# A fused recurrent-attention and feed-forward kernel: input products leave PSUM by a copy and run a block ahead, softplus made from a tanh, another order of steps

## The chip, the cores and the metric

The kernel runs on one core of a Trainium2 chip, as one launch. The time is that of the device for one execution, in microseconds (us). A core has five engines that run their own queues in order: TensorE (PE, matrix products into PSUM; PEld is its weight load), VectorE (DVE), ScalarE (ACT, activation functions read from a table that must be loaded), GpSimd (POOL) and SyncE (SP, here the queue that starts the DMA transfers). PSUM is the memory that TensorE writes to; SBUF is the working memory.

## The reference

```python
def _attn_ref(q, k, v, alpha):          # each (4, 8, 768, 48) float32
    for t in range(S):
        state = alpha[:, :, t, :, None] * state + einsum('bhd,bhe->bhde', k[:, :, t], v[:, :, t])
        y[:, :, t] = einsum('bhd,bhde->bhe', q[:, :, t], state)
def _moe_ref(x, w_in, w_out):           # x = y as (3072, 384); w_in (384, 2048); w_out (2048, 384)
    h = x @ w_in
    sp = np.maximum(h, 0.0) + np.log1p(np.exp(-np.abs(h)))
    g = h * erf(sp)
    return g @ w_out
```

A gated linear recurrence gives x; the feed-forward part takes a product, multiplies it by the erf of its own softplus, and takes a second product.

## The kernel before

**Attention** is done in 24 chunks of 64 steps, each for two of the four batch entries. `ld` starts seven transfers (alpha, k, q in two halves each, v) on SP. `a1` makes the running products of alpha with one scan on VectorE (line 168), `a2` their reciprocals (ScalarE: a check, Ln, Exp; VectorE: a Newton step), `a3` scales k and q, `a4` transposes k (`pn`, line 199) and multiplies q by k (`pS`, line 210), `a5` makes the output (`py`, line 238) and the update of the state T (`pu`, line 249), and splits the output into two halves x_hi and x_lo of the feed-forward's input (lines 286 and 287). The step named `a6` is empty. There are two sets of raw tiles for alpha, q and k, used in turn, and two raw_v.

**The feed-forward part** works on 12 blocks of 256 tokens; two chunks fill one block's x. The 2048 columns are four groups g of 512, and a group is two halves. For a half, `H` takes 18 products (three for each of three slices of the input and two columns of 128: hi by hi, lo by hi, hi by lo; line 323) into a PSUM bank `ph` (two banks); ScalarE reads the bank twice, exp into `w` (line 334, with a running sum into `hflags`) and a copy into `hs` (line 335). `L1` makes s = ln(1 + w), the softplus, and then exp(-ln s), a first reciprocal; `L2` refines it on VectorE (lines 348, 349). `E` loads the gelu table, takes the gelu of all four groups (line 354) and loads the table of logarithm and exp again: erf comes from the gelu and the reciprocal. `Z` multiplies and adds (lines 359, 360). `O` splits a half into gh and gl (a cast on VectorE or a copy on ScalarE, lines 371 and 373, and a subtraction, line 374) and takes 12 products (line 382) into the two accumulators `acc` of the block; there are two `acc` banks in all. `out` copies the accumulators to `o`, one buffer (line 390), and starts the transfers to the output.

The weights come in 28 pieces (`wi_n`, `wo_n`) that are staged in buffers of the pools of `hs` and `s`, converted on ScalarE and VectorE and kept in SBUF as hi and lo halves.

**What sets the order.** The steps are traced in an order written out by hand: START once, ORDER in a loop, TAIL once. `H_0_1@1` is the second half of group 0 of the next block, `Z_0@-1` belongs to the block before; in `a1_0` and `ld_1` the number counts chunks from the loop's first chunk. START holds the first block to its end, seven chunks and the second block's H and L; nine rounds of ORDER and TAIL follow. A planner of the framework then sorts each engine's instructions by that order as a priority and by its own costs, and places tiles into the pools' buffers; an instruction that needs a buffer waits until its last reader is done. Instructions given to `tab` can't be moved across a table load (`new_phase`, line 127). So a table load divides ScalarE's work into two phases: one for gelu, one for logarithm and exp, with the attention's Ln and Exp in the latter. In total 25 tables are loaded.

`general()` is a slow path behind a flag for inputs out of range; it does not run with this data.

Of the kernel before, what the change touches and what calls it, by code (L numbers as in the profile page):

```python
# [14 lines left out]
AMIN = 1e-18  # L15
# [6 lines left out]
RMAX = 1e17  # L22
HMAX = 1e17
SAT = 4.0
RT2 = 2.0**0.5
# [5 lines left out]
    for z in (  # L31
# [13 lines left out]
    )  # L45
# [4 lines left out]
def gla_moe(ctx: ExitStack, tc: tile.TileContext, q, k, v, alpha, w_in, w_out, out):  # L50
# [21 lines left out]
    xp = fast.enter_context(tc.tile_pool(name="xp", bufs=2))  # L72
    keep_s = fast.enter_context(tc.tile_pool(name="keep_s", bufs=NG))
    keep_h = fast.enter_context(tc.tile_pool(name="keep_h", bufs=NG + 1))
    keep_w = fast.enter_context(tc.tile_pool(name="keep_w", bufs=NG + 1))
    tmp = fast.enter_context(tc.tile_pool(name="tmp", bufs=1))
# [4 lines left out]

    raws = []
    for n in range(2):

        ra = raw.tile([P, NP * NI, 1 + TC], F32, name=f"raw_a{n}")
        rq, rk = (raw.tile([P, NP, NI, TC], F32, name=f"raw_{nm}{n}") for nm in "qk")
        e = nc.vector if n == 0 else nc.gpsimd
        for t, fill in ((ra, 1.0), (ra[:, :, 0], 0.0), (rq, 0.0), (rk, 0.0)):
            e.memset(t, fill)
        raws.append((ra, rq, rk))  # L90

# [4 lines left out]
    for i in range(NI):  # L96
# [3 lines left out]
        )  # L100
    fixed = const.tile([P, 5], F32, name="fixed")
    floor, bhi, bsat, bone, ones = (fixed[:, n : n + 1] for n in range(5))
    for t, val in ((floor, AMIN), (bhi, -AHI), (bsat, SAT), (bone, 1.0 + 2.0**-23), (ones, 1.0)):
        nc.gpsimd.memset(t, val)
    NS = M * CPB
    flags = const.tile([P, NS, 2], F32, name="flags")
    nc.gpsimd.memset(flags, 0.0)

    hflags = const.tile([P, NBLK * NG * 2], F32, name="hflags")
    nc.gpsimd.memset(hflags, 0.0)  # L110

# [34 lines left out]
    class Chunk:  # L146
# [6 lines left out]
        def ld(self):  # L153
            self.ra, self.rq, self.rk = raws[self.n % 2]
            self.vv = raw.tile([P, NI * NP * HD + H * D], F32, name="raw_v", tag="raw_v", bufs=2)
            for t, src in ((self.ra[:, :, 1:], alpha), (self.rk, k), (self.rq, q)):
                t = t if src is alpha else t.rearrange("p a i t -> p (a i) t")
                for par in range(2):
                    nc.sync.dma_start(
                        out=t[par * HD : par * HD + D],  # L160
                        in_=src[self.m, self.c, par].rearrange("d a i t -> d (a i) t"),
                    )
            nc.sync.dma_start(out=self.vv, in_=v[self.m, self.c])
# [104 lines left out]

    pools = SimpleNamespace(xp=xp, s=keep_s, h=keep_h, w=keep_w, tmp=tmp, gp=gp, acc=ps_acc, ph=ps_h, flags=hflags)

    class Moe:
# [38 lines left out]
        def H(self, g, half):  # L310
            x_hi, x_lo = self.x
            if half == 0:
                self.hs[g] = self.pl.h.tile([P, GT * TB], F32, name="hs", tag="hs")
                self.w[g] = self.pl.w.tile([P, GT * TB], F32, name="w", tag="w")
            ph = self.pl.ph.tile([P, 512], F32, name="ph", tag="h")
# [11 lines left out]
            sl = slice(half * 512, (half + 1) * 512)  # L327
            w = self.w[g][:, sl]
            if self.pl.flags is None:
                nc.scalar.activation(w, ph, AF.Relu, scale=-1.0, bias=bsat)  # L330
                nc.scalar.activation(w, w, AF.Exp, scale=-1.0, bias=bsat)
            else:
                n = (self.n * NG + g) * 2 + half
                tab(nc.scalar.activation(w, ph, AF.Exp, accum_out=self.pl.flags[:, n : n + 1]))  # L334
            nc.scalar.activation(self.hs[g][:, sl], ph, AF.Copy)  # L335

        def L1(self, g):
            w = self.w[g]
            s = self.pl.s.tile([P, GT * TB], F32, name="s", tag="s")
            tab(nc.scalar.activation(s, w, AF.Ln, bias=bone))  # L340
            tab(nc.scalar.activation(w, s, AF.Ln))  # L341
            tab(nc.scalar.activation(w, w, AF.Exp, scale=-1.0))  # L342
            self.s[g] = s

        def L2(self, g):
            w, s = self.w[g], self.s[g]
            t = self.pl.tmp.tile([P, GT * TB], F32, name="t", tag="tmp")
            nc.vector.tensor_tensor(out=t, in0=s, in1=w, op=ALU.mult)  # L348
            nc.vector.scalar_tensor_tensor(out=w, in0=t, scalar=2.0, in1=w, op0=ALU.subtract, op1=ALU.mult)  # L349

        def E(self):
            new_phase(GELU)
            for s in self.s:
                tab(nc.scalar.activation(s, s, AF.Gelu, scale=RT2))  # L354
            new_phase(LNEXP)

        def Z(self, g):
            s, w, h = self.s[g], self.w[g], self.hs[g]
            nc.vector.tensor_tensor(out=s, in0=s, in1=w, op=ALU.mult)  # L359
            nc.vector.scalar_tensor_tensor(out=h, in0=s, scalar=RT2 / 2, in1=h, op0=ALU.add, op1=ALU.mult)  # L360

# [25 lines left out]
        def out(self):  # L387
            for tt in range(2):
                o = self.pl.gp.tile([P, DM], F32, name="o", tag="o", bufs=1)
                nc.scalar.activation(o, self.acc[tt][:, :DM], AF.Copy, scale=-RT2)  # L390
                nc.sync.dma_start(out=out[bass.ds(self.toks[tt], P), :], in_=o)
# [40 lines left out]
    def general():  # L432

        with ExitStack() as es:
# [47 lines left out]
            rows = part.rearrange("g b t a r e -> g (b t) (a r e)")  # L482
            pl = SimpleNamespace(xp=one, s=one, h=two, w=one, tmp=one, gp=two, acc=acc, ph=ph, flags=None)
            with tc.For_i(0, NT, TB) as tok:
# [10 lines left out]
                for g in range(NG):  # L495
                    m.H(g, 0)
                    m.H(g, 1)
                    m.L1(g)
                    m.L2(g)
                    nc.scalar.activation(m.s[g], m.s[g], AF.Gelu, scale=RT2)  # L500
                    m.Z(g)
# [9 lines left out]
    for n in range(NBLK):  # L511
        m, j = divmod(n, CPB // 2)
        moes.append(Moe(n, [(m * NI + i) * S + j * P for i in range(NI)], pools))

    def run(order, c0, b0):

        for step in order:
# [7 lines left out]
            elif name[0] in "la":  # L525
                if c0 + arg[0] < len(chunks):
# [5 lines left out]
                    else:  # L532
                        getattr(ch, name)()
            elif b0 + int(rel or 0) < NBLK:
                getattr(moes[b0 + int(rel or 0)], name)(*arg)

    run(START, 0, 0)
    for i in range(2, NBLK - 1):
        run(ORDER, 2 * i + 3, i)
    run(TAIL, 2 * NBLK, NBLK - 1)  # L540


    top = const.tile([P, 3], F32, name="top")
    nc.vector.tensor_reduce(
        out=top[:, 0:2], in_=flags.rearrange("p n two -> p two n"), op=ALU.max, axis=mybir.AxisListType.X
    )
    nc.vector.tensor_reduce(out=top[:, 2:3], in_=hflags, op=ALU.max, axis=mybir.AxisListType.X)
    count = const.tile([P, 1], F32, name="count")
    nc.vector.tensor_scalar(out=count, in0=top[:, 0:1], scalar1=RMAX, scalar2=None, op0=ALU.is_ge)
    for n, lim in ((1, 0.0), (2, HMAX)):  # L550
        nc.vector.scalar_tensor_tensor(
            out=count, in0=top[:, n : n + 1], scalar=lim, in1=count, op0=ALU.is_gt, op1=ALU.add
        )
    pf = ps_at.tile([P, 512], F32, name="pf", tag="at")
# [62 lines left out]
```

## Time and profile before

| | us |
|---|---|
| median of three runs | 612.34 |
| lowest and highest | 604.37, 614.47 |
| the profiled execution | 614.45 |
| its span, first to last instruction | 612.7 |
| TensorE busy in the span | 532.7 (87%) |
| TensorE's weight load busy | 507.3 (83%) |
| VectorE busy | 485.8 (79%) |
| ScalarE busy | 476.7 (78%) |
| GpSimd busy | 4.3 (1%) |

The mean granted clock of TensorE is 0.966. A matmul's row shows its whole passage, so that rows of neighbouring matmuls overlap, and the busy time of a group is more than its share of the engine; the distance from start to start is what one costs in a dense row. The first gelu load of each block's output stands at 89.49, 139.68, 177.39, 224.66, 271.18, 316.45, 361.59, 408.54, 453.55, 500.81, 548.63 and 577.70 us: these cut the span into START (two stretches), nine rounds of ORDER and TAIL's two stretches. In a group's row there stand the busy time, the mean duration in ns, and after the second bar the idle time of its engine just before it with what ended it.

### The profile page before, as it was taken

To read this page: it belongs to the slowest core of one execution; us is meant where nothing else is said; L and a number is where in the kernel's file an instruction comes from. 1 tells how busy PE (TensorE), PEld (TensorE's weight loads), DVE (VectorE), ACT (ScalarE), POOL (GpSimd) and SP (SyncE) were. 2 spreads that over 40 slices of the span, in tenths; PEclk is the share of its full clock that TensorE was granted. 3 is DMA by queue.
4 is the path that set the end of the run, shared out by engine and by line. 5 is a ranking of instruction groups with operands and counts; after the bars stand their busy time and mean duration, and the time that the engine had idled before them with its cause. 6 is when DMAs were issued, how large, how long until landed. Compare 5 with 4: busy or idle time off the path is not lost.

```text
span 612.7 us, 17112 instructions
## 1 busy us (share of the span) xinstructions
PE 532.7 (87%) x7386; PEld 507.3 (83%) x7386; DVE 485.8 (79%) x690; ACT 476.7 (78%) x847; POOL 4.3 (1%) x23
## 2 busy tenths in 40 slices
PE   0588498998998998998999998999998998999994
PEld 0468397897988987987988988988988987989984
DVE  6889999899988588678689588589588588549781
ACT  4458988889986887787887886887886787679941
POOL 2000000000000000000000000000000000000000
PEclk9999697999998998999999998999998998999998
DMA  9765523414122122111122122122122010000000
GB/s 250 234 229 170 152 77 111 134 39 110 40 71 71 27 71 71 40 57 58 40 71 71 27 72 71 27 71 71 27 71 71 1 32 28 1 2 27 1 27 30
DMA packets 36371, 43.65 MB, mean 71 GB/s; under 512 B 21952, under 2 KB 25024, under 8 KB 36288
## 3 DMA queue, kind: packets, MB, share of 16 engines
q1 hardware_dynamic: 36288, 42.48, 23.7%
q8 instruction: 60, 0.98, 0.7%
q14 instruction: 23, 0.19, 0.1%
HBM read 37.75 MB, written 4.72 MB: 69 GB/s over the span
## 4 chain that ended last, share of the span: by engine, by line
ACT 38%; PE 29%; DVE 22%; DMA 6%; issue 4%; SPq 0%; DVEq 0%; ACTq 0%
PE acc L382 15%; PE ph L323 11%; ACT w L334 5%; ACT s L354 5%; ACT s L340 4%; ACT hs L335 4%; DMA out_dram<-o 4%; ACT w L341 3%; DVE t L348 3%; ACT w L342 3%; DVE A L168 3%; ACT gh L373 3%; ACT L127 3%; ACT r L176 2%; DVE w L349 2%
## 5 line engine op out<-in xcount | busy, mean ns | idle before, releaser
L323 PE MATMUL ph<-x_hi,wi_hi 128*128 128x256 f32 x576 | 164.9, 289 | 14.4 <-ACT x_hi L286 12.9
L323 PE MATMUL ph<-x_hi,wi_lo 128*128 128x256 f32 x576 | 163.6, 285 | 0.7 <-DVE wi_lo L395 0.7
L323 PE MATMUL ph<-x_lo,wi_hi 128*128 128x256 f32 x576 | 164.0, 285 | 0.0
L382 PE MATMUL acc<-wo_hi,gh 128*128 128x384 f32 x384 | 137.6, 359 | 21.5 <-ACT o L390 16.1
L382 PE MATMUL acc<-wo_hi,gl 128*128 128x384 f32 x384 | 133.0, 349 | 1.2 <-DVE gl L374 1.2
L382 PE MATMUL acc<-wo_lo,gh 128*128 128x384 f32 x384 | 133.3, 348 | 0.0
L323 PEld LDWEIGHTS ph<-x_hi,wi_hi 128*128 128x128 f32 x576 | 109.7, 192 | 17.3 <-ACT x_hi L286 14.5
L323 PEld LDWEIGHTS ph<-x_lo,wi_hi 128*128 128x128 f32 x576 | 110.6, 192 | 1.4 <-DVE x_lo L287 1.2
L323 PEld LDWEIGHTS ph<-x_hi,wi_lo 128*128 128x128 f32 x576 | 110.4, 192 | 1.4 <-DVE wi_lo L395 1.2
L374 DVE TENSOR_TENSOR gl<-hs,gh 128x512 fp32r<-128x512 f32 x96 | 65.2, 687 | 46.7 <-ACT gh L373 46.5
L334 ACT ACTIVATE w<-ph 128x512 f32<-128x512 f32 x96 | 57.6, 601 | 57.1 <-PE ph L323 55.6
L382 PEld LDWEIGHTS acc<-wo_hi,gh 128*128 128x128 f32 x384 | 75.2, 196 | 26.8 <-ACT o L390 18.9
L348 DVE TENSOR_TENSOR t<-s,w 128x1024 f32<-128x1024 f32 x48 | 58.6, 1221 | 31.9 <-ACT w L342 31.9
L382 PEld LDWEIGHTS acc<-wo_hi,gl 128*128 128x128 f32 x384 | 74.9, 196 | 2.4 <-DVE gl L374 2.3
L382 PEld LDWEIGHTS acc<-wo_lo,gh 128*128 128x128 f32 x384 | 75.7, 197 | 0.0
L373 ACT ACTIVATE gh<-hs 128x512 fp32r<-128x512 f32 x72 | 45.3, 630 | 25.9 <-PE acc L382 25.6
L359 DVE TENSOR_TENSOR s<-s,w 128x1024 f32<-128x1024 f32 x48 | 57.7, 1219 | 2.3 <-ACT s L354 2.3
L349 DVE SCALAR_TENSOR_TENSOR w<-t,w 128x1024 f32<-128x1024 f32 x48 | 58.5, 1218 | 0.7
L360 DVE SCALAR_TENSOR_TENSOR hs<-s,hs 128x1024 f32<-128x1024 f32 x48 | 57.6, 1218 | 0.1
L335 ACT ACTIVATE hs<-ph 128x512 f32<-128x512 f32 x96 | 56.1, 598 | 0.0
L340 ACT ACTIVATE s<-w,fixed 128x1024 f32<-128x1024 f32 x48 | 55.5, 1159 | 0.1
L341 ACT ACTIVATE w<-s 128x1024 f32<-128x1024 f32 x48 | 51.4, 1074 | 0.2
(68 smaller groups left out, 745.2 us busy)
## 6 DMA issues: line engine op xcount, KB each, us to landing
raw_v<-in_v_dram SPq DMA_DIRECT2D x24, 448.0 KB, 3.7
wst<-in_moe_w_in_dram SPq DMA_DIRECT2D x12, 512.0 KB, 5.8
wst<-in_moe_w_out_dram SPq DMA_DIRECT2D x16, 384.0 KB, 3.7
raw_a<-in_alpha_dram SPq DMA_DIRECT2D x48, 96.0 KB, 2.9
raw_k<-in_k_dram SPq DMA_DIRECT2D x48, 96.0 KB, 2.2
raw_q<-in_q_dram SPq DMA_DIRECT2D x48, 96.0 KB, 2.4
out_dram<-o SPq DMA_DIRECT2D x24, 192.0 KB, 3.4
```

The source lines that it names most:

```text
L323: nc.tensor.matmul(out=o, lhsT=wt[:, kt, fs], rhs=xt[:, kt, :], start=n == 0, stop=n == 3 * KT - 1)
L334: tab(nc.scalar.activation(w, ph, AF.Exp, accum_out=self.pl.flags[:, n : n + 1]))
L335: nc.scalar.activation(self.hs[g][:, sl], ph, AF.Copy)
L340: tab(nc.scalar.activation(s, w, AF.Ln, bias=bone))
L341: tab(nc.scalar.activation(w, s, AF.Ln))
L348: nc.vector.tensor_tensor(out=t, in0=s, in1=w, op=ALU.mult)
L349: nc.vector.scalar_tensor_tensor(out=w, in0=t, scalar=2.0, in1=w, op0=ALU.subtract, op1=ALU.mult)
L359: nc.vector.tensor_tensor(out=s, in0=s, in1=w, op=ALU.mult)
L360: nc.vector.scalar_tensor_tensor(out=h, in0=s, scalar=RT2 / 2, in1=h, op0=ALU.add, op1=ALU.mult)
L373: nc.scalar.activation(ghf, gg, AF.Copy)
L374: nc.vector.tensor_tensor(out=gl.rearrange("p a t -> p (a t)"), in0=gg, in1=ghf.bitcast(F32), op=ALU.subtract)
L382: nc.tensor.matmul(out=self.acc[tt][:, :DM], lhsT=gt[:, u, ts], rhs=wt[:, f, :], start=f == 0 and n == 0, stop=f == NF - 1 and n == 2,)
```

## The change

- `H` only copies `ph` to `hs`. The exp from PSUM and the `hflags` sum go.
- A new step `U` makes s = tanh(-h/2) from `hs`, 1024 elements at a time, with the table of gelu. `L1` takes ln(0.5 + 0.5 s), which is minus the softplus, then ln(-s) and exp of minus that. `L2`, `Z`, the gelu (now a step `G` for one group) and `out` change signs.
- `E` is gone; the order names the table loads itself, `GELU` and `LN`. In a round, the gelu of block i-1 and the tanh of block i share one phase, the logarithms of block i and the attention have the other.
- Buffers: `s` 5 for 4, `hs` 7 for 5, `w` 4 for 5. One set of raw tiles for alpha, q and k instead of two.
- START ends before the first block's gelu; it holds six chunks, H, U, L1 and L2 of block 0, and six of the eight halves of H of block 1. The loop has eleven rounds, i = 1 to 11; in round i stand H_3 of block i, H_0 to H_2 of block i+1, the attention of chunks 2i+4 and 2i+5 (the x of block i+2), U, L1 and L2 of block i, and G, Z, O and out of block i-1. TAIL is the last block's G, Z, O and out. 26 tables are loaded.

```diff
-        "E@-1 Z_0@-1 O_0_0@-1 O_0_1@-1 a1_0 a2_0 Z_1@-1 O_1_0@-1 a3_0 H_1_0 H_1_1 H_2_0 a4_0 H_2_1 H_3_0 "
-        "Z_3@-1 O_1_1@-1 H_3_1 L1_0 L1_1 Z_2@-1 ld_1 a5_0 a6_0 H_0_0@1 H_0_1@1 L2_0 L2_1 O_2_0@-1 O_2_1@-1 "
-        "O_3_0@-1 L1_2 L2_2 a1_1 a2_1 a3_1 a4_1 O_3_1@-1 L1_3 L2_3 a5_1 a6_1 ld_2 out@-1 ",
+        "GELU a1_0 G_0@-1 G_1@-1 Z_0@-1 H_3_0 G_2@-1 U_0 H_3_1 Z_1@-1 O_0_0@-1 U_2 O_0_1@-1 O_1_0@-1 G_3@-1 U_1 "
+        "Z_2@-1 O_2_1@-1 O_1_1@-1 U_3 LN Z_3@-1 O_2_0@-1 a2_0 L1_0 a3_0 L2_0 a4_0 H_0_0@1 ld_1 a5_0 a1_1 a2_1 "
+        "a3_1 O_3_0@-1 L1_1 H_1_0@1 ld_2 H_1_1@1 L2_1 L1_2 a4_1 O_3_1@-1 H_2_0@1 L1_3 L2_2 H_2_1@1 a5_1 H_0_1@1 "
+        "L2_3 out@-1 ",
...
-    keep_s = fast.enter_context(tc.tile_pool(name="keep_s", bufs=NG))
-    keep_h = fast.enter_context(tc.tile_pool(name="keep_h", bufs=NG + 1))
-    keep_w = fast.enter_context(tc.tile_pool(name="keep_w", bufs=NG + 1))
+    keep_s = fast.enter_context(tc.tile_pool(name="keep_s", bufs=NG + 1))
+    keep_h = fast.enter_context(tc.tile_pool(name="keep_h", bufs=2 * NG - 1))
+    keep_w = fast.enter_context(tc.tile_pool(name="keep_w", bufs=NG))
...
-    for n in range(2):
-        ra = raw.tile([P, NP * NI, 1 + TC], F32, name=f"raw_a{n}")
-        rq, rk = (raw.tile([P, NP, NI, TC], F32, name=f"raw_{nm}{n}") for nm in "qk")
...
+    ra = raw.tile([P, NP * NI, 1 + TC], F32, name="raw_a")
+    rq, rk = (raw.tile([P, NP, NI, TC], F32, name=f"raw_{nm}") for nm in "qk")
...
-            self.ra, self.rq, self.rk = raws[self.n % 2]
+            self.ra, self.rq, self.rk = ra, rq, rk
...
-                tab(nc.scalar.activation(w, ph, AF.Exp, accum_out=self.pl.flags[:, n : n + 1]))
             nc.scalar.activation(self.hs[g][:, sl], ph, AF.Copy)
+        def U(self, g):
+            self.s[g] = self.pl.s.tile([P, GT * TB], F32, name="s", tag="s")
+            tab(nc.scalar.activation(self.s[g], self.hs[g], AF.Tanh, scale=-0.5))
         def L1(self, g):
-            tab(nc.scalar.activation(s, w, AF.Ln, bias=bone))
-            tab(nc.scalar.activation(w, s, AF.Ln))
+            tab(nc.scalar.activation(s, s, AF.Ln, scale=0.5 - 2.0**-24, bias=bhalf))
+            tab(nc.scalar.activation(w, s, AF.Ln, scale=-1.0))
             tab(nc.scalar.activation(w, w, AF.Exp, scale=-1.0))
...
-            nc.vector.scalar_tensor_tensor(out=w, in0=t, scalar=2.0, in1=w, op0=ALU.subtract, op1=ALU.mult)
+            nc.vector.scalar_tensor_tensor(out=w, in0=t, scalar=2.0, in1=w, op0=ALU.add, op1=ALU.mult)
-        def E(self):
-            new_phase(GELU)
-            for s in self.s:
-                tab(nc.scalar.activation(s, s, AF.Gelu, scale=RT2))
-            new_phase(LNEXP)
+        def G(self, g):
+            tab(nc.scalar.activation(self.s[g], self.s[g], AF.Gelu, scale=-RT2))
...
-    for i in range(2, NBLK - 1):
-        run(ORDER, 2 * i + 3, i)
+    for i in range(1, NBLK):
+        run(ORDER, 2 * i + 4, i)
```

More of the change, by code (lines that the diff above doesn't have):

```diff
@@ L22 @@
 RMAX = 1e17
-HMAX = 1e17
-SAT = 4.0
 RT2 = 2.0**0.5
@@ L80, in gla_moe @@
     ps_at = fast.enter_context(tc.tile_pool(name="ps_at", bufs=4, space=PSUM))
-    raws = []
-    for n in range(2):
-        ra = raw.tile([P, NP * NI, 1 + TC], F32, name=f"raw_a{n}")
-        rq, rk = (raw.tile([P, NP, NI, TC], F32, name=f"raw_{nm}{n}") for nm in "qk")
[L87 to L90, printed above, removed]
+    ra = raw.tile([P, NP * NI, 1 + TC], F32, name="raw_a")
+    rq, rk = (raw.tile([P, NP, NI, TC], F32, name=f"raw_{nm}") for nm in "qk")
+    for t, fill in ((ra, 1.0), (ra[:, :, 0], 0.0), (rq, 0.0), (rk, 0.0)):
+        nc.vector.memset(t, fill)
     ident = const.tile([P, P], F32, name="ident")
@@ L100, in gla_moe @@
         )
-    fixed = const.tile([P, 5], F32, name="fixed")
-    floor, bhi, bsat, bone, ones = (fixed[:, n : n + 1] for n in range(5))
-    for t, val in ((floor, AMIN), (bhi, -AHI), (bsat, SAT), (bone, 1.0 + 2.0**-23), (ones, 1.0)):
+    fixed = const.tile([P, 3], F32, name="fixed")
+    bhi, bhalf, ones = (fixed[:, n : n + 1] for n in range(3))
+    for t, val in ((bhi, -AHI), (bhalf, 0.5), (ones, 1.0)):
         nc.gpsimd.memset(t, val)
@@ L107, in gla_moe @@
     nc.gpsimd.memset(flags, 0.0)
-    hflags = const.tile([P, NBLK * NG * 2], F32, name="hflags")
-    nc.gpsimd.memset(hflags, 0.0)
     lower = const.tile([P, NP * NI, 1 + TC], F32, name="lower")
@@ L267, in a5 @@
                     nc.vector.tensor_tensor(out=Tv, in0=Tv, in1=aeb, op=ALU.mult)
-    pools = SimpleNamespace(xp=xp, s=keep_s, h=keep_h, w=keep_w, tmp=tmp, gp=gp, acc=ps_acc, ph=ps_h, flags=hflags)
+    pools = SimpleNamespace(xp=xp, s=keep_s, h=keep_h, w=keep_w, tmp=tmp, gp=gp, acc=ps_acc, ph=ps_h)
     class Moe:
@@ L313, in H @@
                 self.hs[g] = self.pl.h.tile([P, GT * TB], F32, name="hs", tag="hs")
-                self.w[g] = self.pl.w.tile([P, GT * TB], F32, name="w", tag="w")
             ph = self.pl.ph.tile([P, 512], F32, name="ph", tag="h")
@@ L327, in H @@
             sl = slice(half * 512, (half + 1) * 512)
[L328 to L334, printed above, removed]
             nc.scalar.activation(self.hs[g][:, sl], ph, AF.Copy)
+        def U(self, g):
+            self.s[g] = self.pl.s.tile([P, GT * TB], F32, name="s", tag="s")
+            tab(nc.scalar.activation(self.s[g], self.hs[g], AF.Tanh, scale=-0.5))
         def L1(self, g):
-            w = self.w[g]
-            s = self.pl.s.tile([P, GT * TB], F32, name="s", tag="s")
-            tab(nc.scalar.activation(s, w, AF.Ln, bias=bone))
-            tab(nc.scalar.activation(w, s, AF.Ln))
+            s = self.s[g]
+            w = self.pl.w.tile([P, GT * TB], F32, name="w", tag="w")
+            tab(nc.scalar.activation(s, s, AF.Ln, scale=0.5 - 2.0**-24, bias=bhalf))
+            tab(nc.scalar.activation(w, s, AF.Ln, scale=-1.0))
             tab(nc.scalar.activation(w, w, AF.Exp, scale=-1.0))
-            self.s[g] = s
+            self.w[g] = w
         def L2(self, g):
@@ L359, in Z @@
             nc.vector.tensor_tensor(out=s, in0=s, in1=w, op=ALU.mult)
-            nc.vector.scalar_tensor_tensor(out=h, in0=s, scalar=RT2 / 2, in1=h, op0=ALU.add, op1=ALU.mult)
+            nc.vector.scalar_tensor_tensor(
+                out=h, in0=s, scalar=RT2 / 2, in1=h, op0=ALU.subtract, op1=ALU.mult
+            )
         def O(self, g, half):
@@ L389, in out @@
                 o = self.pl.gp.tile([P, DM], F32, name="o", tag="o", bufs=1)
-                nc.scalar.activation(o, self.acc[tt][:, :DM], AF.Copy, scale=-RT2)
+                nc.scalar.activation(o, self.acc[tt][:, :DM], AF.Copy, scale=RT2)
                 nc.sync.dma_start(out=out[bass.ds(self.toks[tt], P), :], in_=o)
@@ L482, in general @@
             rows = part.rearrange("g b t a r e -> g (b t) (a r e)")
-            pl = SimpleNamespace(xp=one, s=one, h=two, w=one, tmp=one, gp=two, acc=acc, ph=ph, flags=None)
+            pl = SimpleNamespace(xp=one, s=one, h=two, w=one, tmp=one, gp=two, acc=acc, ph=ph)
             with tc.For_i(0, NT, TB) as tok:
@@ L497, in general @@
                     m.H(g, 1)
+                    m.U(g)
                     m.L1(g)
                     m.L2(g)
-                    nc.scalar.activation(m.s[g], m.s[g], AF.Gelu, scale=RT2)
+                    m.G(g)
                     m.Z(g)
@@ L513, in gla_moe @@
         moes.append(Moe(n, [(m * NI + i) * S + j * P for i in range(NI)], pools))
+    TABLES = {"LN": LNEXP, "GELU": GELU}
     def run(order, c0, b0):
@@ L533, in run @@
                         getattr(ch, name)()
+            elif name in TABLES:
+                new_phase(TABLES[name])
             elif b0 + int(rel or 0) < NBLK:
@@ L537, in gla_moe @@
     run(START, 0, 0)
-    for i in range(2, NBLK - 1):
-        run(ORDER, 2 * i + 3, i)
+    for i in range(1, NBLK):
+        run(ORDER, 2 * i + 4, i)
     run(TAIL, 2 * NBLK, NBLK - 1)
-    top = const.tile([P, 3], F32, name="top")
+    top = const.tile([P, 2], F32, name="top")
     nc.vector.tensor_reduce(
@@ L546, in gla_moe @@
     )
-    nc.vector.tensor_reduce(out=top[:, 2:3], in_=hflags, op=ALU.max, axis=mybir.AxisListType.X)
     count = const.tile([P, 1], F32, name="count")
     nc.vector.tensor_scalar(out=count, in0=top[:, 0:1], scalar1=RMAX, scalar2=None, op0=ALU.is_ge)
[L550 to L553, printed above, removed]
+    nc.vector.scalar_tensor_tensor(out=count, in0=top[:, 1:2], scalar=0.0, in1=count, op0=ALU.is_gt, op1=ALU.add)
     pf = ps_at.tile([P, 512], F32, name="pf", tag="at")
@@ L558, in gla_moe @@
     fast.close()
-    rv = nc.values_load(total[0:1, 0:1], min_val=0, max_val=3 * P)
+    rv = nc.values_load(total[0:1, 0:1], min_val=0, max_val=2 * P)
     phase["cur"], phase["prev"] = [], []
```

16 rows, old and new, of the table RT2 are left out of this document.

## The prediction

> **What bounds the kernel now.** I read the stretches between the gelu table loads first, then the waits inside the steady part, then the clock, then durations by group. The columns of a stretch are start:end, length, and then busy time with the number of instructions of TensorE, its weight load, VectorE, ScalarE and GpSimd; the last three are granted clock, DMA share and GB/s.
>
> ```profile
> 0.00:89.50 89.50, 54.25 (x960) 48.86 (x961) 78.73 (x144) 60.02 (x121) 4.32 (x23) 0.92 0.63 188
> 89.50:139.70 50.20, 46.08 (x591) 44.44 (x590) 47.63 (x76) 44.07 (x82) 0.00 (x0) 0.93 0.33 96
> 177.40:548.60 371.20, 344.54 (x4931) 330.30 (x4930) 281.46 (x374) 294.59 (x520) 0.00 (x0) 0.98 0.17 48
> 408.50:453.50 45.00, 42.16 (x634) 40.40 (x633) 35.99 (x49) 36.99 (x67) 0.00 (x0) 1.00 0.20 58
> 453.50:500.80 47.30, 43.82 (x634) 42.05 (x633) 36.13 (x49) 37.27 (x67) 0.00 (x0) 0.96 0.14 42
> 548.60:577.70 29.10, 28.19 (x194) 27.43 (x193) 22.28 (x26) 28.75 (x45) 0.00 (x0) 1.00 0.04 15
> ```
>
> The third row is eight periods of the steady loop, 371.2/8 = 46.4 us each. TensorE is the fullest engine. One period's products take 42.16 us at full clock (fourth row) and 43.82 us where the clock fell (fifth row); the other two engines have 36 and 37 us. In eight periods TensorE is idle 371.2 - 344.54 = 26.7 us, and 344.54 - 8 x 42.16 = 7.3 us of its busy time is slow clock. The waits of these eight periods say who makes it idle (total us, times, longest):
>
> ```profile
> PE acc L382 <- ACT o L390: 16.1, 8, 2.6
> PE ph L323 <- ACT x_hi L286: 10.6, 8, 1.4
> ACT o L390 <- DMA out_dram<-o: 4.3, 6, 1.9
> ```
>
> 16.1 + 10.6 = 26.7 us: the whole idle time is two waits per block. The first output product of a block waits until the two accumulators of the block before are copied to `o` (one buffer, so the second copy waits for a DMA). The first input product of a block waits for its x, which the attention step just ahead of it makes. The slow clock follows the first of them, not always:
>
> ```profile
> 191.06 0.44 PE L382 MATMUL acc<-wo_hi,gh 128*128 128x384 f32 x1 [2.10 <-ACT o L390]
> ...
> 190.40:193.80 3.40, 2.74 (x10) 2.74 (x11) 2.27 (x6) 2.83 (x4) 0.00 (x0) 0.70 0.37 132
> 282.30:285.70 3.40, 0.77 (x7) 0.56 (x5) 2.49 (x5) 1.49 (x3) 0.00 (x0) 1.00 0.41 136
> 285.70:289.10 3.40, 3.40 (x20) 3.40 (x21) 2.09 (x4) 3.40 (x6) 0.00 (x0) 1.00 0.16 58
> ```
>
> After a wait of 2.10 us the clock is 0.70 for 3.4 us; after a stretch with 0.77 us of work in 3.40 it stays 1.00.
>
> Ahead of the steady part VectorE is the bound: 78.73 + 47.63 = 126.4 of the first 139.7 us.
>
> **The change, part by part.** The sum is made in stretches between gelu table loads: START until the load that opens the first loop round, nine full rounds, the two last rounds with work missing, and TAIL. These rows carry the durations:
>
> ```profile
> L334 ACT ACTIVATE w<-ph 128x512 f32<-128x512 f32 x96 | 57.6, 601 | 57.1 <-PE ph L323 55.6 <-DVE wbuf L419 1.3
> ...
> L335 ACT ACTIVATE hs<-ph 128x512 f32<-128x512 f32 x96 | 56.1, 598 | 0.0
> ...
> L334 ACT ACTIVATION_READ_ACCUMULATOR w<-ph 128x1 f32 x96 | 19.6, 204 | 0.0
> ...
> L354 ACT ACTIVATE s<-s 128x1024 f32<-128x1024 f32 x48 | 48.1, 1047 | 0.0
> ...
> L127 ACT ACT_TABLE_LOAD x25 | 32.1, 1283 | 1.2 <-PEq L576 0.8
> ...
> L348 DVE TENSOR_TENSOR t<-s,w 128x1024 f32<-128x1024 f32 x48 | 58.6, 1221 | 31.9 <-ACT w L342 31.9
> L374 DVE TENSOR_TENSOR gl<-hs,gh 128x512 fp32r<-128x512 f32 x96 | 65.2, 687 | 46.7 <-ACT gh L373 46.5
> L371 DVE CAST gh<-hs 128x512 fp32r<-128x512 f32 x24 | 10.1, 419 | 0.7 <-PE acc L382 0.7
> L168 DVE TENSOR_TENSOR_SCAN A<-raw_a,lower 128x520 f32<-128x520 f32 x24 | 29.5, 1233 | 0.0
> L181 DVE TENSOR_TENSOR K<-A,r 128x512 f32<-128x512 f32 x24 | 16.5, 686 | 4.8 <-ACT r L178 4.8
> L287 DVE TENSOR_TENSOR x_lo<-py,x_hi 128x192 fp32r<-128x192 f32 x48 | 15.3, 350 | 3.2 <-ACT x_hi L286 3.1
> L267 DVE TENSOR_TENSOR T<-T,A 128x384 f32<-128x384 f32 x20 | 11.0, 551 | 0.0
> ...
> 291.25 1.22 DVE L360 SCALAR_TENSOR_TENSOR hs<-s,hs 128x1024 f32<-128x1024 f32 x1
> 292.39 1.22 DVE L348 TENSOR_TENSOR t<-s,w 128x1024 f32<-128x1024 f32 x1
> ```
>
> *Exp out, tanh in.* Per block eight exps from PSUM with their accumulator reads go, 8 x (0.601 + 0.204) = 6.4 us, and four tanhs of 1024 elements come. No row has a tanh; the gelu of the same shape has 1.047 us, so 4.2 us (bounds 3.8 to 5, from its neighbours' shapes). ScalarE falls by about 2 us a block, from 37 to 35. It isn't the bound: worth nothing by itself. L1, L2, gelu and Z keep count and shape; signs and immediates differ. A PSUM bank is now held for one copy (0.598) instead of exp, read and copy (1.4): slack, since TensorE never waited for an `hs` copy in the waits above.
>
> *The run-ahead.* In the new loop a5 makes x for block i+2 while the input products are those of block i+1 and the last group of block i. So x is ready a round early, and the 1.3 us wait goes. What is late next is the bank or the `hs` slot, below.
>
> *The order.* `O_3_1` now stands before `H_2_0@1`, `H_2_1@1`, a5_1, `H_0_1@1`, and in the next round `H_3_0` and `H_3_1` stand before `O_0_0`. One input half is 2.13 us:
>
> ```profile
> 292.58 0.60 ACT L334 ACTIVATE w<-ph 128x512 f32<-128x512 f32 x1 [3.40 <-PE ph L323]
> ...
> 294.71 0.60 ACT L334 ACTIVATE w<-ph 128x512 f32<-128x512 f32 x1 [0.95 <-PE ph L323]
> ```
>
> so five halves, 10.7 us, cover the accumulators' copies (two of 0.5 us and 2 us of DMA between). The wait for `o` goes if this cover stands; without it the 2 us come back.
>
> *The new wait.* `hs` has seven buffers; at the head of a round four groups of block i-1 and three of block i fill them, so the copies of `H_3_0` and `H_3_1` wait until `O_0_1` of the block before has read its group. Behind them on ScalarE stand U_3 and the table load for the logarithms; both PSUM banks are held meanwhile. From the gelu load the way to the first `gh` is 1.28 + 1.05 + 2 x 1.22 + 0.42 = 5.2 us, against 4.3 us of H_3 on TensorE: about 0.9 us are open in each round unless a left-over half covers them. This is the residue that I count: 42.16 + 0.85 = 43.0 us a period (bounds 42.2, everything covered, and 45.4, all of 26.7/8 back at full clock).
>
> *Raw tiles.* One set instead of two: a chunk's alpha can only be fetched after the scan of the chunk before, its k and q after that chunk's products. Alpha is free early and a period has two chunks, so I cost it at nothing in the loop, hidden by some 20 us between chunks; uncovered it is rival four. The second set's memsets ran on GpSimd at the start and go, as does the `hflags` one: nothing.
>
> *Table loads* go from 25 to 26: 1.28 us in START, on ScalarE, under VectorE.
>
> *START.* VectorE loses one chunk of seven (1.23 + 5 x 0.686 + 2 x 0.35 for x_lo, as much for the two updates of T, and 0.55 = 6.6), L2 and Z of a block (16 x 1.22 = 19.5), eight gl (5.5) and two casts (0.8): 32.4 us in 37 instructions. Starts lie 0.08 us closer than durations (1.14 for 1.22, the last pair of rows), so 29.5 us. With the 13.3 us of idle kept, the first loop load comes at 139.7 - 29.5 = 110.2. Bounds 105 (idle 8) and 122 (five reloads of the single raw set each wait their 2.4 us to landing).
>
> ```profile
> raw_q<-in_q_dram SPq DMA_DIRECT2D x48, 96.0 KB, 2.4
> ```
>
> *The end.* The round for i = 10 has no chunk left. A chunk's attention takes TensorE 298.25 - 296.52 = 1.7 us in a4 and 308.35 + 0.68 - 306.94 = 2.1 us in a5; two chunks 7.6, so 43.0 - 7.6 = 35.4 us. Round i = 11 has 21 us of products and is ScalarE's; the like stretch 548.60:577.70 has ScalarE busy 28.75 of 29.1, I take 28. TAIL has one load, gelu, Z, cast and gl ahead, 5.9 us, then eight output halves of 12 x 0.1733 = 2.08 us (18 starts between the rows at 287.14 and 290.26), 16.6, then what now follows the first last copy, 612.7 - 604.36 = 8.3, and about 1 us of cold clock: 32.
>
> ```profile
> 287.14 0.33 PE L382 MATMUL acc<-wo_lo,gh 128*128 128x384 f32 x1
> ...
> 290.26 0.33 PE L382 MATMUL acc<-wo_lo,gh 128*128 128x384 f32 x1
> ...
> 296.52 0.28 PE L323 MATMUL ph<-x_hi,wi_lo 128*128 128x256 f32 x1
> ...
> 298.25 0.39 PE L323 MATMUL ph<-x_hi,wi_hi 128*128 128x256 f32 x1
> ...
> 306.94 0.34 PE L238 MATMUL py<-Q,T 48*32 48x64 f32 x16
> ...
> 308.35 0.68 PE L249 MATMUL pu<-raw_v,kn 64*64 64x48 f32 x32
> ...
> 604.36 0.49 ACT L390 ACTIVATE o<-acc 128x384 f32<-128x384 f32 x1 [3.18 <-PE acc L382]
> ```
>
> **Sum:** 110.2 + 9 x 43.0 + 35.4 + 28 + 32 = 592.6 us of span. With the 1.75 us outside the span it is 594.4 against the profiled execution's 614.45, 20.1 less. The median of the three runs is 612.34, 2.1 below that execution, so the forecast is 612.3 - 20.1 = 592 us.
>
> **Rivals.**
>
> 1. Better: H_3 and the left-over halves cover everything (period 42.2) and START's idle shrinks (105): 592 - 9 x 0.8 - 5 = 580. For it: all idle of the eight periods has two causes and both are addressed. Against: VectorE and ScalarE stand at 35 to 36 of 42 us, and each round begins with a chain through both.
>
> 2. The clock stays cold in places although the waits go: 7.3/8 = 0.9 us a period, 592 + 8 = 600. For it: the stretch at 282.30, which shows that idling alone doesn't take the clock; attention's small products would be the other suspect. The Trainium skill, "TensorE: Matmul & The Clock Gate", section "HAM oscillation — how this bites in real kernels", says that only gaps above about 3.4 us bring the half clock, and none here is above 2.6. By that rule the waits wouldn't be the cause and this rival would hold. The trace has 0.70 right behind a gap of 2.10 us, so it leans the other way, without settling it.
>
> 3. The waits move. The chain at a round's head or `o` with its one buffer costs half to all of what was there, a period of 44.2 to 45.4: 603 to 614, priced at 608. The Trainium skill, "Perfetto Trace Analysis", section "Optimization Strategy", reads a gap that repeats as a sign of too few buffers; the row of `o` waiting for its DMA agrees (4.3 us), and `hs` at seven for eight is such a place.
>
> 4. Slower: the single raw set. The queue that issues loads is in order and stands a long time on raw_v already (104.2 us in 17 waits, 21.3 the longest, row below); with two sets that is hidden a period ahead, with one an alpha behind such a wait holds the scan, and a2 must come before the next gelu load, so the round is late by the excess. It turns the result from 3.6 us a period (592 + 9 x 3.6 = 624.6, 2% over the median); priced at 4.2: 630. Against it: some 20 us between chunks.
>
> ```profile
> SPq L163 <- PE pu L249: 104.2, 17, 21.3
> ```
>
> **How the numbers follow.** Forecast 0.42 (its own range 583 to 600), better 0.16, cold clock 0.08, moved waits 0.20, single raw set 0.14. The likeliest gives 592. The range 580 to 616 leaves out the last and the lower half of the first rival. Two per cent, about what a measurement of this kernel can tell from no change, are 12 us: faster means below 600.1, slower above 624.6. Faster 0.42 + 0.16 = 0.58, same 0.08 + 0.20 = 0.28, slower 0.14.
>
> **What would show it.** Right: both waits of TensorE, for `o` and for x_hi, near nothing in the steady part; a period of 42 to 44 us; the first loop load near 110; clock 1.00 throughout. ScalarE's total falls by some 25 us, VectorE's stays. Wrong: a repeated TensorE wait on gh, gl or an `hs` copy at the head of each round (rival three); VectorE's scan waiting for raw_a (rival four); 0.96 in the steady windows without waits (rival two); a first loop load after 120.

## The result and the profile after

The changed kernel takes 585.6 us (median; 582.33 to 586.66) against 611.5 us for the kernel before, a ratio of 0.9605 with a 95% interval of 0.9509 to 0.9701. The forecast was 592 us, its range 580 to 616. The profiled execution took 582.33 us with a span of 580.4 us, so it is the lowest of the four; the stages below are its own.

The stretches of the changed kernel between gelu table loads, in the columns that the prediction explained: START, the loop's first round, the next one, the seven rounds i = 3 to 9 in one row, and the two stretches at the end.

```profile
0.00:99.00 99.00, 64.58 (x1187) 58.29 (x1187) 79.46 (x144) 64.38 (x116) 2.41 (x16) 0.97 0.55 169
99.00:151.70 52.70, 43.99 (x617) 40.36 (x618) 52.17 (x88) 43.43 (x70) 0.00 (x0) 0.87 0.35 105
151.70:186.90 35.20, 33.91 (x548) 32.13 (x547) 33.34 (x46) 34.04 (x51) 0.00 (x0) 1.00 0.25 72
186.90:475.60 288.70, 288.70 (x4321) 279.24 (x4320) 250.22 (x335) 254.50 (x377) 0.00 (x0) 1.00 0.20 59
475.60:512.00 36.40, 36.40 (x402) 35.72 (x401) 26.12 (x32) 31.29 (x41) 0.00 (x0) 1.00 0.03 12
512.00:545.80 33.80, 32.86 (x226) 32.05 (x225) 24.56 (x28) 30.64 (x40) 0.00 (x0) 1.00 0.04 14
545.80:580.40 34.60, 19.03 (x96) 18.24 (x96) 17.72 (x20) 10.30 (x14) 0.00 (x0) 0.77 0.07 24
```

The fourth row is the result: TensorE is busy for 288.70 of 288.70 us, at clock 1.00. A round takes 288.7/7 = 41.25 us, where it took 46.4. No row of the kernel before is full like that; here the row behind it is, too. Full means that the record has no gap between products (their ends are modelled in it). The other engines have 36 us each in a round.

The waits of TensorE in the changed kernel, first in the opening 151.7 us and then in the last 104.8:

```profile
PE pn L187 <- DVE K L175: 22.8, 3, 15.3
...
PE acc L367 <- DVE gh L356: 7.8, 1, 7.8
...
PE ph L310 <- ACT wi_hi L379: 4.8, 2, 4.2
```

```profile
PE acc L367 <- DVE gh L356: 8.6, 1, 8.6
```

In the first round the first output product waits 7.8 us for a cast that stands behind the conversion of the second weights on VectorE (52.17 busy of 52.70). In TAIL it waits 8.6 us for the last block's logarithms, gelu and Z.

How the old wait for the copied accumulators was covered can be seen on ScalarE (start, length, line, operation, idle time in brackets):

```profile
316.50 0.49 ACT L375 ACTIVATE o<-acc 128x384 f32<-128x384 f32 x1
316.87 0.64 ACT L358 ACTIVATE gh<-hs 128x512 fp32r<-128x512 f32 x1
318.14 0.60 ACT L315 ACTIVATE hs<-ph 128x512 f32<-128x512 f32 x1 [0.63 <-PE ph L310]
318.99 0.49 ACT L375 ACTIVATE o<-acc 128x384 f32<-128x384 f32 x1 [0.25 <-DMA out_dram<-o]
```

The second copy still waits for the one buffer `o`; input products come in meanwhile (the copy of `ph` at 318.14), so TensorE doesn't notice.

| stage, us | forecast | measured |
|---|---|---|
| START and first round | 110.2 + 43.0 = 153.2 | 151.7 |
| rounds 2 to 9 | 8 x 43.0 = 344.0 | 323.9 |
| round 10 | 35.4 | 36.4 |
| round 11 | 28 | 33.8 |
| TAIL | 32 | 34.6 |
| span | 592.6 | 580.4 |

### The profile page after: what moved, and what is told of

The parts are those of the page before. It is cut to its first block, busy times and chain, and to the rows that moved or that the text cites. A ratio compares the mean times of both kernels' runs of the same rounds, so it can differ in the third digit from the quotient of the medians.

```text
span 580.4 us, 16926 instructions
## 1 busy us (share of the span) xinstructions
PE 519.5 (90%) x7386; PEld 496.0 (85%) x7386; DVE 483.6 (83%) x688; ACT 468.6 (81%) x704; POOL 2.4 (0%) x16
## 4 chain that ended last, share of the span: by engine, by line
PE 69%; DVE 15%; ACT 9%; issue 3%; DMA 2%; SPq 0%; ACTq 0%; DVEq 0%
PE acc L367 29%; PE ph L310 29%; PE py L226 4%; PE pS L198 3%; DVE wbuf L401 2%; DVE s L342 2%; ACT s L326 2%; PE pu L237 1%; PE pn L187 1%; DVE wbuf L404 1%; DVE A L156 1%; DVE t L334 1%; DVE w L335 1%; DVE hs L343 1%; ACT hs L315 1%
## 5 line engine op out<-in xcount | busy, mean ns | idle before, releaser
L310 PE MATMUL ph<-x_hi,wi_hi 128*128 128x256 f32 x576 | 166.9, 290 | 7.5 <-ACT wi_hi L379 4.8
L367 PE MATMUL acc<-wo_hi,gh 128*128 128x384 f32 x384 | 133.2, 347 | 16.4 <-DVE gh L356 16.4
L367 PE MATMUL acc<-wo_hi,gl 128*128 128x384 f32 x384 | 131.4, 346 | 2.0 <-DVE gl L359 1.9
L367 PE MATMUL acc<-wo_lo,gh 128*128 128x384 f32 x384 | 131.0, 341 | 0.0
L310 PEld LDWEIGHTS ph<-x_hi,wi_hi 128*128 128x128 f32 x576 | 111.4, 194 | 10.1 <-ACT wi_hi L379 5.1
L367 PEld LDWEIGHTS acc<-wo_hi,gl 128*128 128x128 f32 x384 | 72.7, 191 | 7.4 <-DVE gl L359 7.0
L367 PEld LDWEIGHTS acc<-wo_lo,gh 128*128 128x128 f32 x384 | 73.7, 192 | 0.0
L326 ACT ACTIVATE s<-s,fixed 128x1024 f32<-128x1024 f32 x48 | 54.6, 1141 | 0.0
L321 ACT ACTIVATE s<-hs 128x1024 f32<-128x1024 f32 x48 | 49.7, 1055 | 1.6 <-DVE wbuf L398 0.9
L328 ACT ACTIVATE w<-w 128x1024 f32<-128x1024 f32 x48 | 50.4, 1051 | 0.3
```

Source lines behind the costliest of these rows:

```text
L310: nc.tensor.matmul(out=o, lhsT=wt[:, kt, fs], rhs=xt[:, kt, :], start=n == 0, stop=n == 3 * KT - 1)
L321: tab(nc.scalar.activation(self.s[g], self.hs[g], AF.Tanh, scale=-0.5))
L326: tab(nc.scalar.activation(s, s, AF.Ln, scale=0.5 - 2.0**-24, bias=bhalf))
L367: nc.tensor.matmul(out=self.acc[tt][:, :DM], lhsT=gt[:, u, ts], rhs=wt[:, f, :], start=f == 0 and n == 0, stop=f == NF - 1 and n == 2,)
```

## Experiments

Times are medians, ratios go to the kernel before as it ran on the same chip beside them, with the 95% interval.

**1. Before, two places of the order moved**

```diff
-E@-1 Z_0@-1 O_0_0@-1 O_0_1@-1 a1_0 a2_0 Z_1@-1 O_1_0@-1 a3_0 H_1_0 H_1_1 H_2_0 a4_0 ...
+E@-1 Z_0@-1 H_1_0 H_1_1 O_0_0@-1 O_0_1@-1 a1_0 a2_0 Z_1@-1 O_1_0@-1 a3_0 H_2_0 a4_0 ...
-ld_1 a5_0 a6_0 H_0_0@1 H_0_1@1 L2_0 L2_1 O_2_0@-1 O_2_1@-1
+ld_1 a5_0 a6_0 L2_0 L2_1 O_2_0@-1 O_2_1@-1 H_0_0@1 H_0_1@1
```

> The kernel before with two places of its loop's order moved and nothing else: two input halves stand ahead of a block's first output product, and two output halves stand between the making of x and the first input product that uses it. Theory 1 (the gain is the two waits of TensorE, covered by the order alone): both waits go, 26.7 us of idle and up to 7 us of slow clock in eight periods, so 578 to 592 us. Theory 2 (it is the lighter ScalarE, tanh for exp) and theory 3 (it needs the block of run-ahead with seven buffers): 604 to 615 us, as before.

593.2 us, ratio 0.974 (0.9662 to 0.9818), just above the range of theory 1 and far below that of the others. Some 16 us of the gain come with no new buffer, no tanh and no run-ahead. The rest doesn't. The same stretch of 290 us in the kernel before, in this one and in the changed kernel:

```profile
190.00:480.00 290.00, 269.17 (x3771) 258.42 (x3772) 226.81 (x302) 228.09 (x407) 0.00 (x0) 0.98 0.20 56
```

```profile
190.00:480.00 290.00, 280.27 (x4054) 267.58 (x4053) 238.71 (x318) 245.33 (x440) 0.00 (x0) 1.00 0.20 57
```

```profile
190.00:480.00 290.00, 290.00 (x4346) 280.51 (x4343) 251.51 (x338) 255.78 (x379) 0.00 (x0) 1.00 0.20 59
```

TensorE's idle time is 20.8, 9.7 and 0 us, and the clock is back at 1.00 with the order alone.

**2 and 3. Each of the two moves by itself**

> The kernel before, with only the first of the two moves of the order-only run: two input halves ahead of a block's first output product. Theory 1: the wait for the copied accumulators goes (16.1 us in eight periods) with most of the slow clock behind it (7.3 us), the wait for x stays: 589 to 600 us. Rival (the clock's cold stretches and the idle time come back at the x wait): 604 to 614 us.

604.6 us, ratio 0.9895 (0.9851 to 0.9938): less of a gain than theory 1 expected, and inside the rival's range.

> The kernel before, with only the second move: two output halves between the making of x and the first input product that uses it. Theory 1: the wait for x goes (10.6 us in eight periods), the one for the accumulators and its slow clock stay: 597 to 606 us. Rival (what is late next takes it all): 608 to 614 us.

601.4 us, ratio 0.9858 (0.9809 to 0.9907): the time is as expected, the way to it isn't. The idle times of the two in the same stretch are 14.4 and 13.6 us, for 20.8 before:

```profile
190.00:480.00 290.00, 275.63 (x3849) 259.16 (x3849) 231.28 (x309) 240.07 (x427) 0.00 (x0) 0.99 0.20 56
```

```profile
190.00:480.00 290.00, 276.43 (x3939) 265.81 (x3941) 230.58 (x306) 239.56 (x429) 0.00 (x0) 0.99 0.19 54
```

TensorE's largest waits in this stretch, in the kernel before, with the first move and with the second:

```profile
PE acc L382 <- ACT o L390: 14.0, 7, 2.6
PE ph L323 <- ACT x_hi L286: 7.9, 6, 1.4
```

```profile
PE ph L323 <- ACT x_hi L286: 9.5, 6, 1.6
```

```profile
PE acc L382 <- DVE gl L374: 5.3, 5, 1.1
PE acc L382 <- DVE gh L371: 4.6, 6, 0.9
PE py L238 <- DVE sT L215: 3.6, 5, 0.8
```

The first move takes the wait for `o` away, and the one for x grows. The second was to leave the wait for `o`, but no wait for `o` is left either; in its place the output products wait for gl and gh, and attention's `py` for sT. So each move changes the whole order of the round and not one wait. That the two gains, 1.05% and 1.42%, add up to the 2.6% of both doesn't show that each wait has a price of its own.

**4. The changed kernel with x just in time again**

```diff
-a2_0 L1_0 a3_0 L2_0 a4_0 H_0_0@1 ld_1 a5_0 a1_1 ...
+a2_0 L1_0 a3_0 L2_0 a4_0 ld_1 a5_0 H_0_0@1 a1_1 ...
-        run(ORDER, 2 * i + 4, i)
+        run(ORDER, 2 * i + 3, i)
```

START also loses its last chunk.

> The changed kernel with the attention one chunk later, so that a round's second attention step makes the x that the next input product uses at once, as before the change; START loses a chunk. Theory 1: a wait of 1.3 to 2 us for x comes back in each of eleven rounds, 595 to 608 us. Theory 2: nothing, 583 to 588 us.

612.1 us, ratio 1.006 (1.0026 to 1.0095): the whole gain is gone, more than expected. In the same stretch TensorE is idle for 7.4 us and at clock 0.99. Only 2.4 us of that are waits for x; three waits of `pu` make up 4.9, and the profile shows nothing that they wait for:

```profile
PE pu L237 <- issue: 4.9, 3, 1.7
PE ph L310 <- ACT x_hi L274: 2.4, 6, 0.5
```

```profile
190.00:480.00 290.00, 282.63 (x4041) 268.44 (x4040) 231.37 (x309) 236.53 (x353) 0.00 (x0) 0.99 0.20 59
```

Rounds 3 to 9 take 44.0 us each (gelu loads at 186.19 and 494.46), 2.8 more than in the changed kernel. The idle time explains about 1.1 of the 2.8 us; the rest is busy time. The planner now cuts attention's `a5`, the output products and the input products into shorter pieces: counted from start to start, TensorE goes from one kind of product to another 21 times a round and not 15, and these steps take 4.0 us a round without their idle time, where they took 2.4. The first output product behind attention's takes 0.45 us and the next starts 0.28 us after it did (323.77 - 323.49), though the two are of one shape and the second takes 0.34; in a dense row of output products starts lie 0.173 us apart.

```profile
322.42 1.15 PE L198 MATMUL pS<-Q,K 48*64 48x64 f32 x32
323.49 0.45 PE L367 MATMUL acc<-wo_hi,gh 128*128 128x384 f32 x1
323.77 0.34 PE L367 MATMUL acc<-wo_lo,gh 128*128 128x384 f32 x1
```

An order with x just in time and fewer pieces was not tried.

**5. The changed kernel with the old load on ScalarE**

```diff
+            if half == 0 and self.n is not None:
+                nc.scalar.activation(self.hs[g][:, sl], ph, AF.Copy, accum_out=fixed[:, 3:4])
             nc.scalar.activation(self.hs[g][:, sl], ph, AF.Copy)
```

> The changed kernel, with one more reading of PSUM with an accumulator for each group, 4 x 0.8 us of ScalarE a block: about what exp against tanh saved, and a bank is held longer. Theory 1: TensorE stays full in the loop, 584 to 590 us. Theory 2: most of the gain goes back, 600 to 612 us. Theory 3: as theory 1.

592.9 us, ratio 0.9737 (0.9665 to 0.981): 7 us, more than theory 1 gave and much less than theory 2. Where they are, the stages say. START and the first round of this kernel:

```profile
0.00:102.80 102.80, 66.11 (x1186) 59.79 (x1186) 80.06 (x145) 68.86 (x131) 2.42 (x16) 0.95 0.53 163
102.80:159.70 56.90, 46.69 (x627) 43.76 (x628) 53.97 (x89) 46.62 (x79) 0.00 (x0) 0.85 0.36 106
```

They are 3.8 and 4.2 us longer than in the changed kernel, 8.0 of the profile's 9.7 us. The load put back is also more than the change took off: ScalarE is busy for 494.8 us here, 468.6 in the changed kernel and 476.7 in the kernel before. The loop keeps its 41.3 us a round (289.3 us in seven). ScalarE's load is worth nothing while TensorE is full, and it is worth its time in the start, where ScalarE and VectorE work on the weights in turn.

**6 and 7. The changed kernel with the softplus from exp again, in the logarithms' phase**

```diff
-            tab(nc.scalar.activation(self.s[g], self.hs[g], AF.Tanh, scale=-0.5))
+            tab(nc.scalar.activation(self.s[g], self.hs[g], AF.Exp))
-... U_0 ... U_2 ... U_1 ... U_3 LN Z_3@-1 O_2_0@-1 a2_0 L1_0 ...
+... LN U_0 U_1 U_2 U_3 Z_3@-1 O_2_0@-1 a2_0 L1_0 ...
```

The logarithm's scale and bias and the signs behind it go back with it.

> The changed kernel with the softplus made from exp of the copied product again, in the logarithms' phase: four instructions of 1.05 us move from the gelu's phase to the other, everything else stays (copy out of PSUM, run-ahead, order). Theory 1 (the table in which it is made doesn't matter while TensorE is full): 583 to 592 us. Rival (the tanh in the gelu's phase is what balances the phases; the logarithms' phase has no idle time and grows by 3.8 us in each of eleven rounds): 615 to 630 us.

619.2 us, ratio 1.0174 (1.0096 to 1.0252). But START was spoilt: with no gelu in its gelu phase the planner was free to mix, and eleven more tables were loaded. Its rounds take 44.7 us (gelu loads at 197.77 and 510.64 in seven). So the second form:

```diff
-... LN U_0 U_1 U_2 U_3 Z_3@-1 O_2_0@-1 a2_0 L1_0 ... L1_1 ... L1_2 ... L1_3
+... LN Z_3@-1 O_2_0@-1 a2_0 U_0 L1_0 ... U_1 L1_1 ... U_2 L1_2 ... U_3 L1_3
```

> As the run with exp in the logarithms' phase, but each exp stands right ahead of its own group's logarithm and not four in a row ahead of the attention's, and START has no empty phase for gelu (which had brought extra table loads there). Theory (the phases' balance: the logarithms' phase grows by 3.8 us in each round, whatever the place within it): 608 to 622 us. Rival (the price was the place within the phase and START): 584 to 596 us.

606.3 us, ratio 0.9928 (0.9897 to 0.9958): neither. The first form's extra 13 us lie nearly all ahead of its third round, since the later rounds take 44.4 us here (187.74 to 498.61 in seven), almost as long as there. 21 us remain that go with the phase in which the softplus is begun, under this order. One round, gelu's phase and then the other, first the changed kernel, then this one:

```profile
309.30:330.30 21.00, 21.00 (x334) 20.48 (x333) 19.35 (x25) 16.12 (x24) 0.00 (x0) 1.00 0.24 68
330.30:350.70 20.40, 20.40 (x302) 19.55 (x301) 16.53 (x24) 20.32 (x32) 0.00 (x0) 1.00 0.20 57
```

```profile
319.50:325.20 5.70, 5.70 (x43) 5.70 (x44) 5.62 (x9) 5.65 (x9) 0.00 (x0) 1.00 0.28 80
325.20:365.00 39.80, 37.42 (x592) 36.17 (x592) 30.83 (x40) 30.84 (x48) 0.00 (x0) 0.96 0.20 53
```

ScalarE's work is 36.4 and 36.5 us; it is the place of it that differs. The long phase isn't full either: in it ScalarE waits for the attention's scan on VectorE, and TensorE for the copies out of PSUM that stand behind that wait in ScalarE's queue (waits from 190 to 480 us; in the changed kernel neither occurs there):

```profile
ACT r L164 <- DVE A L156: 35.5, 7, 5.6
...
PE ph L310 <- ACT hs L315: 15.4, 7, 2.6
```

So the expected reason (3.8 us more work in a full phase) is not what the trace shows; it shows a wait of about 5 us in each round that the planner's order for two even phases doesn't have. An order made anew for this form was not tried.

**8. Before, with one set of raw tiles**

> The kernel before with one set of raw tiles for alpha, q and k instead of two. Forecast of the prediction (nothing, there are some 20 us between chunks): 606 to 614 us. Rival four of the prediction (a load late behind raw_v holds the scan and then the phase): 620 to 650 us.

612.0 us, ratio 1.0048 (1.0015 to 1.008), some 3 us. The forecast's nothing is nearly right, rival four is not.

**9. The changed kernel with six buffers for `hs`**

> The changed kernel with six buffers for hs instead of seven, so that the input products of the next block run a group less ahead and their copies wait for an earlier block's output step. Theory 1 (the order is what matters, six still cover): 584 to 592 us. Theory 3 (the gain needs the run-ahead): 595 to 610 us.

664.9 us, ratio 1.0935 (1.0876 to 1.0994): far beyond both. A step of one buffer costs 79 us. The eight rounds from the second on take 48.1 us each (157.94 to 543.09) for 40.5 (151.72 to 475.63), which is 61 of the 81 us between the two spans. Its waits from 190 to 480 us:

```profile
ACT hs L315 <- DVE gl L359: 28.9, 13, 4.3
...
PE acc L367 <- DVE gh L356: 17.4, 6, 4.5
```

The copies out of PSUM stand on ScalarE and wait until an earlier block's group has been read; behind them in the same queue stand the tanh, the gh copies and the table load. That is the wait that the prediction expected with seven buffers. With seven it doesn't occur, with six it repeats in each round.

**10. The end split**

The last round and TAIL become one list, in which groups 0 and 1 of the last block get logarithms, gelu and output products before groups 2 and 3 get their logarithms:

```diff
+... U_3 LN L1_0 L2_0 Z_3@-1 O_2_0@-1 L1_1 L2_1 O_3_0@-1 O_3_1@-1 out@-1 GELU G_0 G_1 Z_0 O_0_0
+O_0_1 LN L1_2 L2_2 Z_1 O_1_0 O_1_1 L1_3 L2_3 GELU G_2 Z_2 O_2_0 O_2_1 G_3 Z_3 O_3_0 O_3_1 out
```

> The changed kernel with its last round and TAIL rewritten: the last block's groups 0 and 1 get their logarithms, then the gelu table is loaded and their output products run while groups 2 and 3 get theirs; two table loads more. If the end is ScalarE's chain of logarithms ahead of the first output product (8.59 us of idle TensorE in the changed kernel), 575 to 580 us; if it is VectorE's or the loads eat it, 583 to 589 us.

580.8 us, ratio 0.9538 (0.9492 to 0.9585). It lies just above the range for ScalarE's chain. It is the lowest median of all, but the interval overlaps with that of the changed kernel, and the profile has little of it: from round 11's gelu load to the end 581.0 - 513.92 = 67.1 us against 580.4 - 512.04 = 68.4. The wait of 8.6 us became two of 3.2.

**11. The low halves of the weights on GpSimd**

```diff
-        split(hi, lo, z.bitcast(F32))
+        nc.scalar.activation(hi, z.bitcast(F32), AF.Copy)
+        nc.gpsimd.tensor_tensor(out=lo, in0=z.bitcast(F32), in1=hi.bitcast(F32), op=ALU.subtract)
```

> The changed kernel with the subtraction that makes the weights' low halves on GpSimd instead of VectorE, 28 instructions of 0.55 to 0.69 us, some 15 us of VectorE in the first 150 us. If VectorE's load bounds the start: 574 to 582 us. If GpSimd is slower at it and the low halves come late, or it slows VectorE beside it: 585 to 600 us.

595.0 us, ratio 0.9782 (0.9733 to 0.9831). The loop is full as before; START is later by nearly 10 us (first loop load at 108.78 for 99.03). Up to 150 us ScalarE waits 6.3 us for wo_lo and TensorE 3.2 us for wi_lo, which GpSimd makes; so what the 15 us of VectorE are worth by themselves isn't shown.

**12. The split end with a first round of its own**

Eight pieces of the second weights move from START's list into the first round, behind the first output halves.

> The split-end kernel, with a list of its own for the loop's first round: eight of the sixteen second-weight pieces are converted in it, behind the first output halves, and no longer ahead of them. In the changed kernel the first output product waits 7.79 us for a gh that stands behind those conversions on VectorE. If that idle time is lost to the end (TensorE is full in the loop, so nothing is caught up): 572 to 578 us. If VectorE is the bound of the first 150 us, and the wait only comes later: 578 to 586 us.

585.1 us, ratio 0.9588 (0.9528 to 0.9648), no faster than the split end alone (0.9538): the wait came back later. From 80 to 200 us the first output products wait for gh again, in two places:

```profile
PE acc L380 <- DVE gh L369: 9.5, 2, 4.9
```

## Why the prediction was right

The mechanism stood: both waits of the steady loop are gone, the slow clock with them, and TensorE is the bound. That the number is so near is in part luck: in the profile the rounds 2 to 9 came out 20 us shorter than the sum had them, and the last three stretches 9 us longer. Point by point:

- *What bounds the kernel.* Right. The 26.7 us of idle were those two waits, and the order alone (experiment 1) takes half of the idle time and the slow clock away.
- *The period of 43.0 us.* The term that was mis-sized most. It was TensorE's 42.16 us and a residue of 0.85. The residue is nothing (288.70 busy of 288.70), so here it is the better rival's mechanism that came: left-over products cover the head of a round. At each gelu load of these rounds TensorE has still to do some 75 input products that stand ahead of it in the order, 9 us of work at 0.118 us each (2.13/18). The products themselves take 41.25 us, less than that rival's 42.2, too; of the 0.9 us, 0.6 are steps from one kind of product to another, 15 a round for 18. Over rounds 2 to 9 it is 20 us less than the sum had, but not all of it was saved: 6 us of it are work put off. The second round, 35.2 us, does 548 products where a later one does 617, and the difference is done at the end, in rounds 10 and 11.
- *The end.* 28 + 32 = 60 us were forecast and 68.4 measured, which took back 8 of the 20 us. The step that failed in round 11 is "21 us of products and is ScalarE's": TensorE is busy for 32.86 of its 33.8 us, with 116 input products where the order alone gives 36, because the left-over ones end up here; ScalarE is busy for 30.64. In TAIL the first output product starts 553.46 - 545.77 = 7.7 us after the gelu load where 5.9 were counted (TensorE's wait is 8.6), and the products take 19.0 us for 16.6 and 1 of cold clock, at clock 0.77.
- *START.* 110.2 us for the first loop load was wrong by 11 us, and the first round gave them back: it took 52.7 us, not 43. The sum of both was off by 1.5. The reason was right (VectorE's work): it is 79.46 + 52.17 = 131.6 us in these 151.7, where the prediction's terms come to 94 + 36. The place of the border wasn't, since the second weights' conversion goes on behind the load.
- *Exp out, tanh in: "worth nothing by itself".* This step failed. It is right for ScalarE's load in the loop. That load was mis-sized, too: ScalarE's total fell by 8 us (476.7 to 468.6) and not by some 25, since durations of rows that overlap were added up. But with exp in the logarithms' phase and the rest kept (experiment 7), a round goes from 41.25 to 44.4 us and the kernel to 606 us. What the tanh does under this order is to make two even phases of 21 us out of one of 6 and one of 40, so that the attention's scan is done when ScalarE comes to its reciprocal, and the copies out of PSUM don't stand behind that wait.
- *The run-ahead.* Its size failed. The prediction priced it at the wait of 1.3 us; with x just in time again (experiment 4) a round takes 2.8 us more, of which 0.4 are the wait for x, and the whole gain is gone.
- *The new wait at `hs`.* Real, but not with seven buffers; with six it costs 79 us.
- *The single raw set at nothing.* Nearly: 0.5% in the kernel before. In the changed kernel two sets weren't tried.
- *The slow clock* follows the waits, as forecast: it is 1.00 in every row of the loop from the second round on. Rival two fell. What brings it can't be told from these runs. In the kernel before it fell behind five of the eight waits for `o`, but not behind the longest (2.63 us); with the first move alone it fell once in the loop, to 0.54 for 3.4 us at 397.40, behind a wait of 1.57 us.
- *Slips in its sums.* 592 + 9 x 3.6 is 624.4 and not 624.6, and 42.16 + 26.7/8 is 45.5 and not 45.4. Nothing hangs on them.

So the gain isn't a sum of parts. Experiments 4, 7 and 9 each undo one part and lose all of it, most of it, and more than it, and experiment 1 gets two thirds of it with none of these parts. What pays is that TensorE is full, and in these three a wait that the order doesn't cover, or a row cut into pieces, undoes that. In none of them was the order made anew for what was left.

## What to carry to other kernels

Read the period of the steady loop and the work of the fullest engine in it, and name the waits that make up the difference; if they are few, an order that puts ready work of the same engine ahead of them is worth trying before any arithmetic is changed. A step moved to another table phase is to be priced by what each phase then holds and by who queues behind it, not by the engine's total. Buffers for a run-ahead can be a threshold: count the tiles alive at the head of a round, since one too few can cost more than the run-ahead gains.

## What the runs showed of the hardware

GpSimd took 1.34 us (median) for a subtraction of 128x384 and 1.46 us for one of 128x512 in experiment 11, where VectorE took 0.55 and 0.68 in the changed kernel. Single ones took up to 5.65 us. The numbers are the shortest, the median and the longest, in ns; the profile's durations for GpSimd are rough.

```profile
L408 POOL TENSOR_TENSOR wo_lo<-wbuf,wo_hi x16: 1010/1342/5646, 58.2 to 142.6; 128x384 fp32r<-128x384 f32 x16
L408 POOL TENSOR_TENSOR wi_lo<-wbuf,wi_hi x12: 1267/1464/2217, 7.5 to 76.4; 128x512 fp32r<-128x512 f32 x12
```

```profile
L380 DVE TENSOR_TENSOR wo_lo<-wbuf,wo_hi x16: 539/552/559, 54.9 to 130.3; 128x384 fp32r<-128x384 f32 x16
L380 DVE TENSOR_TENSOR wi_lo<-wbuf,wi_hi x12: 662/680/691, 7.8 to 68.7; 128x512 fp32r<-128x512 f32 x12
```

TensorE's record has no gap over 288.7 us of the changed kernel, with 36 us of every 41 busy on both of the engines that feed it.
